# Folds of three Fourier transforms dealt out anew between VectorE and GpSimd, with their steps spread

## The chip, the cores and the metric

The kernel runs on one core of a Trainium2 chip. The metric is device microseconds (us) of one execution. Before the change three runs took 786.69, 786.71 and 786.85 us, median 786.71 us.

## The reference

Attention with a few sink tokens and a sliding window, then a Fourier mix, a normalisation and a feed-forward layer; 4 batches, 8 heads, 768 tokens, 64 features a head, model width 512, hidden width 2048, all float32.

```
scores = q @ k.T / sqrt(64);  keep = (key < n_sink) | (0 <= query - key < window)    # n_sink 4, window 128
a = softmax(where(keep, scores, -1e9));  x = heads side by side of (a @ v)           # (4, 768, 512)
u = x + real(fft(fft(x, axis=1), axis=2))
un = (u - mean(u)) / sqrt(var(u) + 1e-6)
out = u + relu(un @ w_ch1) @ w_ch2
```

## The kernel before

**Attention.** A block is 128 queries of one batch; there are 24 blocks, and each is worked in four steps of two heads. A hand-written loop runs over the steps s, and in every step each engine gets its instructions in the order of a table (SCHEDULE). Two steps' scores are issued together (TensorE, L702) into score buffers of which there are two. VectorE moves the older window's scores over (merge, L708), adds the mask and takes the maximum (soft1, L720). ScalarE takes the exponential (L726) two steps later. TensorE turns the probabilities (L751), ScalarE copies them out (pta, L758), GpSimd masks the newer and the older block (ptl at L767, pta at L775) five steps behind, and TensorE forms the products with v (xt, L789) seven steps behind. GpSimd also makes the sink weights (sk, L737 and L738), TensorE turns them (L809), ScalarE copies them (skt, L814) before a score buffer is used again. Once per block VectorE inverts the sums (L742, L743) and stores the block (L819).

**The transform.** The real part of the transform over 768 tokens and 512 features uses symmetry: before TensorE multiplies by cosines and sines, the data is folded. Of the six blocks of a batch, block j and block 3+j are added (the even token fold) and subtracted (the odd token fold, both L351), for j = 0, 1, 2. Each result is then folded over features: the even one in place (L361, the even feature fold), the odd one into the other half of the same tile (L358, the odd feature fold). ScalarE rounds the tile to its high part (gh, L364), VectorE keeps the low part (gl, L367). One middle row goes its own way: it is read from DRAM, put in place of row 0 of block 3 (put_row, L380), folded (mid_sum, L371), and split into a high and a low part (sph, mid_row, L375 and L377). Then follow the products of the first stage (L394), of the second (L421, L442), the sums d (L447, L448) and the updates of u (L458, L459), which for the first two batches are on GpSimd.

**What sets the order.** When the fourth block of batch b has been stored (step 24b + 25), fourier() enters each of its instructions in a list of events: so many steps later, on such an engine. The table SCHEDULE says where in an engine's row of a step the events stand ("V", "G", "A", "T"). For j the folds count from k = 0, 4, 8; the first stage's products begin at step 15. Up to step 97 the instructions stand on their engines as written; from there on the tile framework's scheduler orders them. The fourth transform (b = 3, called tail) has its folds on VectorE alone, and lies in that part. The first three transforms fold at about 48 to 72, 95 to 126 and 154 to 190 us.

The odd token fold has one buffer, the even one two. Instructions of one engine run in their order, so one that waits holds all behind it.

Of the kernel before, what the change touches and what calls it, by code (L numbers as in the profile page):

```python
# [25 lines left out]
NHALF = NB // 2  # L26
# [8 lines left out]
NR = 33  # L35
# [23 lines left out]
WARM = 11  # L59
WARM_STEP = (8, 0, 8, 4, 8, 4, 0)  # L60
FILL_AT, FILL = (24, 36), 0
FOLD_AT, FOLD_LAST, FOLD_ENG = (0, 4, 8), (0, 4, 8), "VG"

F_N, F_M, F_S, ROW = (3, 3), (4, 5), (6, 7), (5, 8, 10)
EV_A = 0

SINK0_AT = 3, 3, "V"
# [138 lines left out]
def kernel(  # L206
# [15 lines left out]
    V, A, G, T = nc.vector, nc.scalar, nc.gpsimd, nc.tensor  # L222

    def f32(ap):
        return ap.bitcast(F32)
# [44 lines left out]
    def run(general):  # L270
        tag = "g" if general else ""
        with ExitStack() as p1:
# [8 lines left out]
            def at(s, eng, fn):  # L281
                ev.setdefault((s, eng), []).append(fn)
# [26 lines left out]
            sph = fpool.tile([P, 384], F32R, name="sph")  # L309
# [22 lines left out]
            def fourier(b, at, ready):  # L332
# [5 lines left out]
                t_ = {}  # L338
# [9 lines left out]
                def fold_n(eng, j, odd):  # L348
                    t = fw.tile([P, DM], F32, tag=f"f{odd}", name=f"f{odd}_{b}_{j}", bufs=2 - odd)
                    t_["eo", j, odd] = t  # L350
                    eng.tensor_tensor(t, u[j], u[NHALF + j], op=ALU.subtract if odd else ALU.add)  # L351

                def fold_m(eng, j, odd):

                    g = t_["eo", j, 0]
                    if odd:
                        t = t_.pop(("eo", j, odd))
                        eng.tensor_tensor(g[:, 257:512], t[:, 1:256], t[:, 511:256:-1], op=ALU.subtract)  # L358
                        t_["g", j] = t_.pop(("eo", j, 0))
                    else:  # L360
                        eng.tensor_tensor(g[:, 1:256], g[:, 1:256], g[:, 511:256:-1], op=ALU.add)  # L361

                def fold_hi(j):
                    A.copy(gh[:, j], t_["g", j])  # L364

                def fold_lo(j):
                    V.tensor_tensor(gl[:, j], t_.pop(("g", j)), f32(gh[:, j]), op=ALU.subtract)  # L367
# [2 lines left out]
                    r = t_["x0"]  # L370
                    V.tensor_tensor(r[:, 1:256], r[:, 1:256], r[:, 511:256:-1], op=ALU.add)  # L371

                def mid_row():
                    t = t_["x0"]
                    V.tensor_copy(sph[:NR, :257], t[:, :257])  # L375
                    lo = sph[NR - 1:NR, :257]
                    V.tensor_tensor(lo, t[NR - 1:NR, :257], f32(lo), op=ALU.subtract)  # L377

# [84 lines left out]
                tail = b == B - 1 or general  # L463
                at(1, "S", load_row)
                for j in range(NHALF):
                    k = ready[j]
                    e0, e1 = FOLD_TAIL if tail else FOLD_ENG
                    eng = {"V": V, "G": G}
                    at(k + F_N[0], e0, lambda j=j: fold_n(eng[e0], j, 0))
                    at(k + F_N[1], e1, lambda j=j: fold_n(eng[e1], j, 1))  # L470
                    at(k + F_M[0], e0, lambda j=j: fold_m(eng[e0], j, 0))
                    at(k + F_M[1], e1, lambda j=j: fold_m(eng[e1], j, 1))
                    at(k + F_S[0], "A", lambda j=j: fold_hi(j))
                    at(k + F_S[1], "V", lambda j=j: fold_lo(j))
                at(ready[0] + ROW[0], "V", put_row)
                at(ready[0] + ROW[1], "V", mid_sum)
                at(ready[0] + ROW[2], "V", mid_row)
                k = ready[2] + S1
                n1, na, nb = PARTS_TAIL if tail else PARTS[b]
                for i, (kind, mc) in enumerate((("a", 0), ("a", 1), ("r", 0), ("b", 0), ("b", 1))):  # L480
# [152 lines left out]
            hp = []  # L633

            def window_attention(fourier, load_constants):
                with ExitStack() as pa:
                    kpool = pa.enter_context(tc.tile_pool(name="kpool", bufs=1, side="right"))
# [189 lines left out]
                    with ExitStack() as man:  # L827
# [130 lines left out]
                        while s < last:  # L958
# [25 lines left out]
                            for e in "AVGT":  # L984
                                for op in SCHEDULE[s >= PHASE][e][k]:
                                    if op in EVENTS:
                                        if (s, op) == (4, "G"):
                                            load_constants()
                                        run_ev(s, op)
                                    elif op in STEP_LAG:  # L990
                                        lag(table[op], s, STEP_LAG[op])
                                    else:
                                        at_ = s - BLOCK_AT[op]
                                        if at_ % NP == 0 and 0 <= at_ // NP < NQ:
                                            table[op](at_ // NP)
                                            if op == "store_x" and at_ // NP % NB == 3:
                                                b = at_ // NP // NB
                                                fourier(b, lambda d, e, f, s=s: at(s + d, e, f), FOLD_AT if b < B - 1 else FOLD_LAST)
                            s += 1
                    extra.clear()  # L1000
                return last

            def general_attention(fourier):
                for b in range(B):
                    u = uview(b)
# [331 lines left out]
```

## Time and profile before

| | |
|---|---|
| profiled execution | 786.78 us |
| its span, first to last instruction | 784.9 us |
| mean granted TensorE clock | 0.993 |
| TensorE (PE) busy | 755.2 us, 96% |
| VectorE (DVE) busy | 460.6 us, 59% |
| ScalarE (ACT) busy | 239.0 us, 30% |
| GpSimd (POOL) busy | 177.6 us, 23% |

A busy share is an average over the whole span. Attention and transforms fill the first 222 us, the feed-forward layer the rest, so the question in which stage an engine waits is answered by rows of that stage. A row of the timeline has the start in us, the duration in us, the engine, the line, the operation, output and input, and in brackets the idle time before it and what ended it. A row of the waits has who waited for whom, us in total, times and longest. A row of groups has the busy us and the mean ns behind the bar, then idle time before. Rows of one engine can overlap a little, since an instruction begins before the one ahead has drained. In a row of a stretch of time, busy times of PE, PEld (weight loads), DVE, ACT and POOL are followed by the granted clock, the DMA share and GB/s.

### The profile page before, as it was taken

What the parts mean: (1) busy time and instruction counts of PE and PEld (TensorE: products, weight loads), DVE (VectorE), ACT (ScalarE), POOL (GpSimd) and SP (SyncE); (2) the same over time, 40 slices, a digit from 0 to 9 for tenths busy, and PEclk for the clock granted to TensorE, in tenths of its full rate; (3) what the DMA queues carried; (4) which work ended last, traced back from release to release, by engine and by line L of the source; (5) the groups of instructions that cost most, each with busy time, mean ns of one, the idle gap of its engine ahead of it and who ended that gap; (6) DMA issues with size and microseconds to landing.
All of it is one profiled execution on the core that took longest, in us unless ns stands there. A gap on an engine that the chain in (4) does not pass through costs nothing.

```text
span 784.9 us, 11953 instructions
## 1 busy us (share of the span) xinstructions
PE 755.2 (96%) x4379; PEld 615.8 (78%) x4379; DVE 460.6 (59%) x1354; ACT 239.0 (30%) x704; POOL 177.6 (23%) x283
## 2 busy tenths in 40 slices
PE   7999998988899999999999999999999999999996
PEld 5666876866778878899888888888888888888895
DVE  6788687999999589561356424662456425611211
ACT  4887765756633133221111111111111110110110
POOL 2566477476645255200000000000000000000000
PEclk9999999999999999999999999999999999999999
DMA  9853525433305366120100002000200001000100
GB/s 311 251 171 109 140 84 176 127 112 99 131 27 159 111 196 210 62 71 1 54 1 0 1 9 99 1 1 0 81 1 0 1 0 54 1 1 0 55 1 32
DMA packets 41812, 57.69 MB, mean 74 GB/s; under 512 B 2796, under 2 KB 27500, under 8 KB 41360
## 3 DMA queue, kind: packets, MB, share of 16 engines
q1 hardware_dynamic: 41456, 53.07, 21.7%
q0 software_dynamic: 288, 3.76, 1.2%
q8 instruction: 37, 0.61, 0.3%
q14 instruction: 31, 0.25, 0.1%
HBM read 47.37 MB, written 9.45 MB: 72 GB/s over the span
## 4 chain that ended last, share of the span: by engine, by line
PE 80%; DVE 13%; issue 2%; POOL 1%; ACT 1%; DMA 1%; SPq 0%; DVEq 0%; ACTq 0%; POOLq 0%
PE h L619 33%; PE o L1124 33%; PE xt L789 3%; PE s L702 3%; DVE sm L720 2%; PE pt L751 2%; DVE cv L591 1%; PE za L394 1%; DVE s L708 1%; DVE cv L590 1%; PE a L421 1%; DVE cv L592 1%; DVE f L351 1%; PE x L801 1%; DMA vt<-in_v_sink_dram 1%
## 5 line engine op out<-in xcount | busy, mean ns | idle before, releaser
L1124 PE MATMUL o<-w,h 128*128 128x512 f32 x876 | 216.5, 394 | 0.0
L1117 DVE SCALAR_TENSOR_TENSOR h<-h,h 128x512 fp32r<-128x512 f32 (+1 forms) x107 | 65.4, 611 | 247.7 <-ACT h L1112 247.5
L1124 PEld LDWEIGHTS o<-w,h 128*128 128x128 f32 x876 | 162.8, 188 | 35.5
L1112 ACT ACTIVATE h<-h 128x512 fp32r<-128x512 f32 (+1 forms) x107 | 57.2, 535 | 366.4 <-PE h L619 360.1
L619 PE MATMUL h<-un_slots,w 128*128 128x512 f32 (+1 forms) x576 | 124.7, 365 | 0.0
L619 PEld LDWEIGHTS h<-un_slots,w 128*128 128x128 f32 x576 | 99.6, 188 | 19.6
L619 PE MATMUL h<-un_last,w 128*128 128x512 f32 (+1 forms) x432 | 89.0, 355 | 0.0
L619 PEld LDWEIGHTS h<-un_last,w 128*128 128x128 f32 x432 | 72.7, 188 | 12.8
L726 ACT ACTIVATE sm<-sm,mx 128x132 f32<-128x132 f32 x192 | 75.8, 400 | 7.1 <-DVE mx L720 7.1
L1148 DVE STREAM_TRANSPOSE unf<-un 32x128 f32<-32x128 f32 x224 | 67.7, 302 | 3.2
L702 PE MATMUL s<-ring,q 64*128 64x260 f32 x320 | 51.2, 422 | 12.2 <-DVE mx L720 6.4
L720 DVE CUSTOM_DVE_ANT_0 sm<-s,mask 128x132 f32<-128x132 f32 x192 | 48.7, 292 | 9.3 <-ACT skt L814 2.7
L702 PEld LDWEIGHTS s<-ring,q 64*128 64x128 f32 x320 | 27.1, 188 | 28.2 <-issue 12.4
L608 POOL TENSOR_TENSOR w<-cv,w 128x512 fp32r<-128x512 f32 x25 | 33.9, 1354 | 35.5 <-ACT w L607 35.4
L789 PE MATMUL xt<-ptl,ldv 128*64 128x128 f32 x384 | 38.9, 288 | 0.0
L708 DVE COPY_PREDICATED s<-older,s 128x256 f32<-128x256 uint8 x80 | 33.6, 420 | 7.2 <-ACT skt L814 6.8
L726 ACT ACTIVATION_READ_ACCUMULATOR sm<-sm,mx 128x1 f32 x192 | 36.8, 192 | 0.0
L1124 PE MATMUL o<-w_ring,h 128*128 128x512 f32 x144 | 35.6, 393 | 0.0
L767 POOL TENSOR_SCALAR_AFFINE_SELECT ptl<-pta 128x512 f32<-128x512 f32 x48 | 32.2, 672 | 14.4 <-ACT pta L758 14.4
L789 PEld LDWEIGHTS xt<-ptl,ldv 128*64 128x64 f32 x384 | 21.6, 137 | 14.9 <-issue 8.1
L789 PE MATMUL xt<-pta,ldv 128*64 128x128 f32 x320 | 31.7, 277 | 0.2 <-POOL pta L775 0.2
L751 PE MATMUL pt<-ident,sm 128*128 128x128 f32 x192 | 31.6, 288 | 0.0
(200 smaller groups left out, 1040.9 us busy)
## 6 DMA issues: line engine op xcount, KB each, us to landing
raw<-in_moe_w_ch_dram SPq DMA_DIRECT2D x32, 512.0 KB, 3.7
ldv<-in_v_dram SPq DMA_DIRECT2D x28, 256.0 KB, 3.6
ring<-in_qk_dram SPq DMA_DIRECT2D x24, 264.0 KB, 4.6
out_dram<-u SPq DMA_DIRECT2D x24, 256.0 KB, 3.8
q<-in_qk_dram SPq DMA_DIRECT2D x20, 256.0 KB, 4.2
cst<-in_dft_dram POOLq DMA_DIRECT2D x1, 3348.0 KB, 11.7
ud<-us SPq DMA_DIRECT2D x12, 256.0 KB, 2.2
u<-ud SPq DMA_DIRECT2D x2, 1024.0 KB, 5.1
```

The source lines that it names most:

```text
L608: G.tensor_tensor(d[1], tf, f32(d[0]), op=ALU.subtract)
L619: T.matmul(ps[:, :tb], a[:, cs], x[:, :, cc, :], start=n == 0, stop=n == 3 * NCC - 1)
L702: T.matmul(ps[:, j, :P + W], st["q", g][rows, hp, :], keys(g, 2 * hp + j), start=True, stop=True)
L708: V.copy_predicated(ps[:, :, P + NS:P + W], older[qi > 2], ps[:, :, 0:P])
L720: V.tensor_tensor_reduce(sm[:, h % 4], ps[:, j, P:P + W], mask[min(qi, 3)], -SCALE, 3.0e38, ALU.add, ALU.min, accum_out=mx[:, 0, h:h + 1])
L726: A.activation(sm[:, h % 4], sm[:, h % 4], AF.Exp, bias=mx[:, 0, h:h + 1], scale=-1.0, accum_out=mx[:, 1, h:h + 1])
L751: T.transpose(ps[:, j], sm[:, j, NS:], ident)
L789: T.matmul(ps[D * j:D * j + D, p, :], st["v", kb(g) - i][:, h, :], a[:, h % 4, :], start=i == 0, stop=i == n - 1)
L1112: A.activation(h[0], ps[:, :tb], AF.Relu)
L1117: V.scalar_tensor_tensor(h[1], ps[:, :tb], 0.0, f32(h[0]), op0=ALU.max, op1=ALU.subtract)
L1124: T.matmul(po[i], a[:, ts_], x, start=f == 0 and n == 0, stop=f == NF - 1 and n == 2)
L1148: V.transpose(unf[32 * q:32 * q + 32, :, r], un[r].rearrange("p (c q j) -> p c q j", c=NCC, q=4)[:, :, q])
```

## The change

For the first three transforms both token folds go to GpSimd and both feature folds to VectorE (before: the even ones on VectorE, the odd ones on GpSimd). The odd token fold stands one step after the even one. For j = 0 and 1 the odd feature fold, the high part and the low part come one step later than before; for j = 2 they keep their steps. The high part of the middle row goes to ScalarE, one step earlier, its low part stays on VectorE, three steps later. The fourth transform keeps its engines; its odd token fold moves by a step, and its middle row is split in the same manner.

```diff
-FOLD_AT, FOLD_LAST, FOLD_ENG = (0, 4, 8), (0, 4, 8), "VG"
-F_N, F_M, F_S, ROW = (3, 3), (4, 5), (6, 7), (5, 8, 10)
+FOLD_AT, FOLD_LAST, FOLD_ENG = (0, 4, 8), (0, 4, 8), "GV"
+F_STEPS = ((3, 4), (4, 5), (6, 7)), ((3, 4), (4, 6), (7, 8))
+ROW = 5, 8, 9, 13
...
-                def mid_row():
+                def mid_hi():
+                    A.copy(sph[:NR, :257], t_["x0"][:, :257])
+
+                def mid_lo():
                     t = t_["x0"]
-                    V.tensor_copy(sph[:NR, :257], t[:, :257])
                     lo = sph[NR - 1:NR, :257]
                     V.tensor_tensor(lo, t[NR - 1:NR, :257], f32(lo), op=ALU.subtract)
...
+                    f_n, f_m, f_s = F_STEPS[0 if tail or j == NHALF - 1 else 1]
                     e0, e1 = FOLD_TAIL if tail else FOLD_ENG
-                    at(k + F_N[0], e0, lambda j=j: fold_n(eng[e0], j, 0))
-                    at(k + F_N[1], e1, lambda j=j: fold_n(eng[e1], j, 1))
-                    at(k + F_M[0], e0, lambda j=j: fold_m(eng[e0], j, 0))
-                    at(k + F_M[1], e1, lambda j=j: fold_m(eng[e1], j, 1))
-                    at(k + F_S[0], "A", lambda j=j: fold_hi(j))
-                    at(k + F_S[1], "V", lambda j=j: fold_lo(j))
+                    at(k + f_n[0], e0, lambda j=j: fold_n(eng[e0], j, 0))
+                    at(k + f_n[1], e0, lambda j=j: fold_n(eng[e0], j, 1))
+                    at(k + f_m[0], e1, lambda j=j: fold_m(eng[e1], j, 0))
+                    at(k + f_m[1], e1, lambda j=j: fold_m(eng[e1], j, 1))
+                    at(k + f_s[0], "A", lambda j=j: fold_hi(j))
+                    at(k + f_s[1], "V", lambda j=j: fold_lo(j))
                 at(ready[0] + ROW[0], "V", put_row)
                 at(ready[0] + ROW[1], "V", mid_sum)
-                at(ready[0] + ROW[2], "V", mid_row)
+                at(ready[0] + ROW[2], "A", mid_hi)
+                at(ready[0] + ROW[3], "V", mid_lo)
```

Line numbers in the changed kernel are larger by 2 at the folds (L353 token folds, L363 and L360 feature folds, L369 low part, L381 the row's low part) and by 6 in the attention (L773, L781 masks, L743, L744 sink weights, L714 merge, L825 store).

GpSimd at the first transform's folds j = 0 and 1, before (f0 is an even fold's tile and f1 an odd one's, u0 the batch's blocks, pta and ptl the probabilities, sk the sink weights):

```order
L767 AFFINE_SELECT ptl_5_3_830<-pta_5_3_801 128x512
L351 TENSOR_TENSOR f1_0_0_832<-u0_64 128x512
L775 AFFINE_SELECT pta_5_3_801<-pta_5_3_801 128x512
L737 CAST sk_6_809<-sm_6_2_778 128x2x16
L738 TENSOR_TENSOR sk_6_809<-sm_6_2_778,sk_6_809 128x2x16
L767 AFFINE_SELECT ptl_6_1_882<-pta_6_1_860 128x512
L358 TENSOR_TENSOR f0_0_0_823<-f1_0_0_832 128x255
L737 CAST sk_7_912<-sm_7_0_826 128x2x16
L738 TENSOR_TENSOR sk_7_912<-sm_7_0_826,sk_7_912 128x2x16
L767 AFFINE_SELECT ptl_6_3_934<-pta_6_3_903 128x512
L351 TENSOR_TENSOR f1_0_1_936<-u0_64 128x512
```

And the same place now:

```order
L773 AFFINE_SELECT ptl_5_3_828<-pta_5_3_801 128x512
L353 TENSOR_TENSOR f0_0_0_830<-u0_64 128x512
L781 AFFINE_SELECT pta_5_3_801<-pta_5_3_801 128x512
L353 TENSOR_TENSOR f1_0_0_865<-u0_64 128x512
L743 CAST sk_6_809<-sm_6_2_778 128x2x16
L744 TENSOR_TENSOR sk_6_809<-sm_6_2_778,sk_6_809 128x2x16
L773 AFFINE_SELECT ptl_6_1_882<-pta_6_1_858 128x512
L743 CAST sk_7_911<-sm_7_0_824 128x2x16
L744 TENSOR_TENSOR sk_7_911<-sm_7_0_824,sk_7_911 128x2x16
L773 AFFINE_SELECT ptl_6_3_931<-pta_6_3_901 128x512
L353 TENSOR_TENSOR f0_0_1_933<-u0_64 128x512
L353 TENSOR_TENSOR f1_0_1_965<-u0_64 128x512
```

The odd token fold stands behind the older block's mask and ahead of the sink weights; the feature fold behind the next mask is gone; at j = 1 the two token folds follow one another.

VectorE at the second transform, before (the inverse of a block, then the burst of four that ends with the token fold of j = 2, then the merge):

```order
L742 TENSOR_SCALAR mx_13_1512<-mx_13_1512 128x8
L743 RECIPROCAL mx_13_1512<-mx_13_1512 128x8
L375 CAST sph_88<-xr_1_1440 33x257
L377 TENSOR_TENSOR sph_88<-xr_1_1440,sph_88 1x257
L367 TENSOR_TENSOR gl_1_1429<-f0_1_1_1654,gh_1_1428 128x512
L351 TENSOR_TENSOR f0_1_2_1778<-us_1_2_1072,us_1_5_1075 128x512
L708 COPY_PREDICATED s_15_0_1769<-older1_122,s_15_0_1769 128x2x128
```

VectorE now, one step later, behind the next step's softmax:

```order
L369 TENSOR_TENSOR gl_1_1429<-f0_1_1_1660,gh_1_1428 128x512
L363 TENSOR_TENSOR f0_1_2_1783<-f0_1_2_1783 128x255
L825 TENSOR_TENSOR u2_65<-x_12_1801,mx_12_1385 128x512
L360 TENSOR_TENSOR f0_1_2_1783<-f1_1_2_1821 128x255
L381 TENSOR_TENSOR sph_88<-xr_1_1440,sph_88 1x257
L714 COPY_PREDICATED s_15_2_1825<-older1_122,s_15_2_1825 128x2x128
```

The low part, and the row's, have moved behind the softmax of two steps, to the even feature fold and the store that stood there already, and the odd feature fold has come from GpSimd; behind the inverse only the odd feature fold of j = 1 is left.

GpSimd at the same place now (L462 and L463 are updates of the batch before):

```order
L773 AFFINE_SELECT ptl_13_3_1781<-pta_13_3_1751 128x512
L353 TENSOR_TENSOR f0_1_2_1783<-us_1_2_1069,us_1_5_1072 128x512
L781 AFFINE_SELECT pta_13_3_1751<-pta_13_3_1751 128x512
L462 TENSOR_TENSOR u0_64<-u0_64,d_0_1_1650 128x257
L463 TENSOR_TENSOR u0_64<-u0_64,d_0_1_1650 128x255
L353 TENSOR_TENSOR f1_1_2_1821<-us_1_2_1069,us_1_5_1072 128x512
L743 CAST sk_14_1759<-sm_14_2_1728 128x2x16
```

The odd token fold, which VectorE's odd feature fold of the next step reads, has been put behind the two updates.

## The prediction

> **What bounds the kernel now.** I read the page first (one core, clock 0.993), then TensorE's waits, then VectorE, GpSimd and TensorE in order of time where the three transforms fold: 48 to 72, 95 to 126 and 154 to 190 us.
>
> ```profile
> PE 755.2 (96%) x4379; PEld 615.8 (78%) x4379; DVE 460.6 (59%) x1354; ACT 239.0 (30%) x704; POOL 177.6 (23%) x283
> ...
> PE s L702 <- DVE mx L720: 4.5, 9, 2.3
> PE s L702 <- PE pt L751: 1.7, 2, 1.0
> PE s L702 <- DVE mx L742: 1.7, 4, 1.1
> PE s L702 <- DVE d L448: 1.2, 1, 1.2
> PE b L442 <- ACT asb L430: 1.0, 1, 1.0
> PE a L421 <- DVE mx L742: 0.8, 1, 0.8
> PE unx L544 <- DVE u L819: 0.7, 1, 0.7
> ```
>
> TensorE is the bound over the whole span. The waits (us in total, times, longest), taken from 48 to 190 us, add to 11.6 us: nearly all are scores waiting for VectorE to have freed a score buffer. So here VectorE sets the end, and only some 11.6 us can be won.
>
> What makes VectorE late are bursts, and GpSimd inside them. Alone, a token fold on VectorE lasts 0.64 us and a feature fold 0.42; next to GpSimd they do not:
>
> ```profile
> 48.52 0.64 DVE L351 TENSOR_TENSOR f<-u 128x512 f32<-128x512 f32 x1
> 110.78 0.42 DVE L361 TENSOR_TENSOR f<-f 128x255 f32<-128x255 f32 x1
> 115.00 0.65 DVE L375 CAST sph<-xr 33x257 fp32r<-33x257 f32 x1
> 115.69 0.74 DVE L377 TENSOR_TENSOR sph<-xr,sph 1x257 fp32r<-1x257 f32 x1
> 116.46 1.01 DVE L367 TENSOR_TENSOR gl<-f,gh 128x512 fp32r<-128x512 f32 x1
> 117.39 1.76 DVE L351 TENSOR_TENSOR f<-us,us 128x512 f32<-128x512 f32 x1
> 119.07 0.41 DVE L708 COPY_PREDICATED s<-older,s 128x256 f32<-128x256 uint8 x1
> ...
> 50.62 1.27 POOL L351 TENSOR_TENSOR f<-u 128x512 f32<-128x512 f32 x1
> 51.85 0.82 POOL L775 TENSOR_SCALAR_AFFINE_SELECT pta<-pta 128x512 f32<-128x512 f32 x1
> 52.62 0.21 POOL L737 CAST sk<-sm 128x32 fp32r<-128x32 f32 x1
> 53.77 0.72 POOL L358 TENSOR_TENSOR f<-f 128x255 f32<-128x255 f32 x1
> 116.90 1.70 POOL L351 TENSOR_TENSOR f<-us,us 128x512 f32<-128x512 f32 x1
> ```
>
> Columns are start and duration. In the second transform the fold that starts on VectorE at 117.39 ends at 119.15. GpSimd's fold ends at 118.60, and 118.60 plus about 0.6 is 119.2; GpSimd's own 1.70 is 1.27 plus what was left of VectorE's low part, 0.4 (to 116.46 + 1.01 = 117.47, where rows of one engine overlap by 0.1). So a VectorE instruction with two operands in SBUF and a GpSimd instruction take turns, whole instruction by whole instruction. [...]
>
> **The change part by part.** Over the three transforms VectorE's rows are:
>
> ```profile
> L361 DVE TENSOR_TENSOR f<-f 128x255 f32<-128x255 f32 x9 | 5.3, 592 | 0.0
> L351 DVE TENSOR_TENSOR f<-u 128x512 f32<-128x512 f32 x6 | 5.0, 832 | 0.0
> L351 DVE TENSOR_TENSOR f<-us,us 128x512 f32<-128x512 f32 x3 | 3.5, 1172 | 0.0
> L375 DVE CAST sph<-xr 33x257 fp32r<-33x257 f32 x3 | 1.4, 481 | 0.0
> ```
>
> - Removed from VectorE: nine token folds, 8.5 us with their waits (9 x 0.64 = 5.8 alone), and three casts, 1.4 us. Added: nine odd feature folds, 9 x 0.42 = 3.8 us alone. So VectorE gains between 3.4 us (5.8 + 1.4 - 3.8) and 6.1 us (8.5 + 1.4 - 3.8), before new waits.
> - GpSimd: nine odd feature folds go (0.72), nine even token folds come (1.27): 9 x 0.55 = 5.0 us more. Nine long instructions more stand in VectorE's way.
> - ScalarE: three casts of 33x257, no more than the 0.65 us of the slowest one on VectorE, one of them per transform in an engine that is busy 30%: cost between 0 and 2 us, taken at 0, since in one row alone of those above (1.0 us) TensorE waits for ScalarE. The fourth transform gets its cast off VectorE too: -0.2 us taken, 0 to -0.7.
> - New order: the odd token fold now stands a step later on GpSimd, ahead of the sink weights; the last steps of a transform put low part, even feature fold, store, odd feature fold and the middle row's low part in one row on VectorE. No DMA moves with the folds. In the part that is ordered by the scheduler, from the fourth transform on, one row load and one weight load each change places with a block's store in SP's queue; taken at 0, as three weights are kept in flight (up to one of VectorE's conversions late if they were not), and two of TensorE's products change places with their neighbours.
>
> First transform. Its rows, VectorE then TensorE:
>
> ```profile
> 51.54 0.63 DVE L361 TENSOR_TENSOR f<-f 128x255 f32<-128x255 f32 x1
> 52.70 0.40 DVE L380 COPY u<-xr 1x512 f32<-1x512 f32 x1
> 53.03 0.41 DVE L708 COPY_PREDICATED s<-older,s 128x256 f32<-128x256 uint8 x1
> 65.98 0.90 DVE L361 TENSOR_TENSOR f<-f 128x255 f32<-128x255 f32 x1
> 66.80 0.68 DVE L819 TENSOR_TENSOR us<-x,mx 128x512 f32<-128x512 f32 x1
> 67.40 0.41 DVE L708 COPY_PREDICATED s<-older,s 128x256 f32<-128x256 uint8 x1
> ...
> 54.11 0.71 PE L702 MATMUL s<-ring,q 64*128 64x260 f32 x4
> 68.58 0.71 PE L702 MATMUL s<-ring,q 64*128 64x260 f32 x4
> 120.19 0.71 PE L702 MATMUL s<-ring,q 64*128 64x260 f32 x4 [2.31 <-DVE mx L720]
> 124.90 1.15 PE L702 MATMUL s<-ring,q 64*128 64x260 f32 x8
> ```
>
> GpSimd's first fold (50.62) becomes the even one; the feature fold wanted at 51.54 waits for its end at 51.89, then for the mask of the older block, which GpSimd has started by then: 52.5. The odd fold follows on GpSimd, from about 52.8 to 54.05. The row's copy into the block (L380) overwrites what both folds read, so it cannot start before 54.05, and the merge behind it moves from 53.03 to 54.4: +1.35, which the scores at 54.11 feel. From start to start a feature fold takes 0.35 (0.42 less the overlap), the store 0.6 (66.80 to 67.40), a low part 0.6 like a token fold of its size. VectorE then skips a low part and a token fold (1.2 us) for a feature fold: 1.35 - 1.2 + 0.35 leaves 0.5 us, which I carry into the last burst. Instead of 65.98 to 67.40 (1.4 us) stand: low part 0.6 after about 0.7 of an odd token fold, even feature fold 0.35 after a sink cast (0.2), store 0.6, odd feature fold 0.35 and the row 0.35, between them a short sink instruction (0.2) and a mask (0.6): 3.95 us, +2.5. The merge of 67.40 comes at about 70.4 and the scores of 68.58 at about 71.6: **+3.0 us** (1.3 if only the row's wait stays, 4.7 if the clock drops as below).
>
> Second transform. The four VectorE rows from 115.00 take 4.07 us to 119.07; what is left there is one feature fold, so the merge comes at about 116.4, 2.7 us earlier, and TensorE's 2.31 us wait at 120.19 goes. But one step on, ScalarE's copy of the sink weights (117.25) still holds the softmax to about 118.6. [...] After today's wait the clock falls:
>
> ```profile
> 117.25 0.27 ACT L814 CAST skt<-s 128x128 fp32r<-128x128 f32 x1 [1.47 <-PE s L809]
> ...
> 120.00:122.00 2.00, 1.62 (x10) 0.69 (x10) 1.97 (x10) 1.64 (x8) 1.92 (x5) 0.85 0.00 0
> 122.00:124.00 2.00, 2.00 (x18) 1.67 (x18) 1.79 (x12) 0.00 (x0) 1.85 (x5) 0.50 0.00 0
> 124.00:126.00 2.00, 2.00 (x14) 1.30 (x14) 0.62 (x2) 1.57 (x3) 1.77 (x4) 0.79 0.43 138
> ```
>
> The column after POOL's is the granted clock: 0.85, 0.50, 0.79 over 6 us, which costs 0.3 + 1.0 + 0.4 = 1.7 us. [...] I take **-0.3 us** (-2.7 if the clock stays up, +0.7 if it falls as before). [...]
>
> Third transform. The same shape: a gain at the bursts ahead of the softmax, given back at the last one, where two updates again stand ahead of the odd token fold:
>
> ```profile
> 176.66 0.42 DVE L708 COPY_PREDICATED s<-older,s 128x256 f32<-128x256 uint8 x1
> 180.94 0.42 DVE L708 COPY_PREDICATED s<-older,s 128x256 f32<-128x256 uint8 x1
> ```
>
> The burst ahead of 176.66 loses the same four instructions as the one ahead of 119.07. Of that head start the sink copy, which holds the second step's softmax as above, leaves between 1.1 and 2.5 us (2.3 of 2.7 there). The last burst costs 2.5 more, as in the first transform, so the merge of 180.94 moves by 0 to 1.4 us: **+0.6 us**. Two refinements are left out, the statistics of the first batch that run between, and the conversions of weights behind.
>
> Sum: 3.0 - 0.3 + 0.6 - 0.2 = **+3.1 us**. The profiled execution took 786.78 us (span 784.9; the median is 786.71), so 789.9.
>
> **The rivals.** (1) Faster: GpSimd gets ahead, since it loses the feature folds that sat between its masks. If each odd token fold is over before VectorE wants it (about 1.3 us earlier than I place it), the bursts cost their price alone: the second transform keeps its 2.3 us and the 1.7 us of clock, the first loses 0.8: 786.78 - 4.0 + 0.8 = 783.6. For it: GpSimd is busy in 23% of the span. Against: in the three rows with the clock above it is busy for 1.92, 1.85 and 1.77 of 2.00 us. (2) GpSimd becomes the bound: its 5.0 us more reach TensorE through the masks, 791.8; against it, the masks run two steps ahead of their products. (3) The waits only change places, each giving back what it took: 786.8.
>
> **How the numbers follow.** The forecast has 0.42, its own range 787.6 to 792.4 (the first transform's term from 1.3 to 4.7, the third's from 0 to 1.4); rival 1 has 0.30, since the relief of VectorE is certain and the new waits are replayed; rival 2 0.12; rival 3 0.16. Within 0.2% (1.6 us) is what a measurement can't tell from no change. So slower 0.42 + 0.12 = 0.54, same 0.16, faster 0.30. The range 783.2 to 792.4 takes in rival 1 but for its lowest third and leaves out about a tenth on either side.
>
> **What would show it.** The row's copy waiting for GpSimd near 54 us; feature folds far above 0.42 us at the end of each transform; no VectorE burst and no 2.31 us wait near 118 us, but a wait at the scores two steps later. Wrong if the last-burst feature folds take 0.42, or if TensorE's waits from 48 to 190 us fall well below 11.6 us.

## The result: 7.6 us slower, and the profile after

The changed kernel takes 794.31 us in the median of five runs (792.47 to 795.54), the kernel before 786.71 beside it. The ratio is 1.0094 (95% interval 1.008 to 1.0108). The prediction said 789.9, with 783.2 to 792.4 as its range: the direction holds, the size does not. The profiled execution took 794.31 us at a granted clock of 0.987, with a span of 792.6 us (784.9 before).

The page's row of busy times first, then TensorE's waits from 48 to 200 us (us in total, times, longest):

```profile
PE 758.1 (96%) x4379; PEld 619.4 (78%) x4379; DVE 456.0 (58%) x1350; ACT 239.7 (30%) x708; POOL 181.5 (23%) x283
```

```profile
PE s L708 <- issue: 8.2, 5, 2.2
PE s L708 <- DVE mx L726: 2.0, 6, 1.1
PE unx L550 <- DVE u L825: 1.9, 1, 1.9
PE s L708 <- DMA ldv<-in_v_dram: 1.2, 1, 1.2
PE b L446 <- ACT asb L434: 1.0, 1, 1.0
PE s L708 <- DVE mx L748: 0.7, 3, 0.2
...
```

VectorE is 4.6 us less busy and GpSimd 3.9 us more, and TensorE waits longer: 15.7 us, with three rows of 0.3 us and less that are left out above, where all rows of before add to 12.0 from 48 to 200 us. That is half of the 7.7 us by which the span grew. The other half shows in the granted clock. Narrow windows find its edges; the rows below are cut at them. Columns: window and its length, busy time of PE, PEld, DVE, ACT and POOL, granted clock, then the DMA share and rate.

```profile
69.44:72.85 3.41, 1.47 (x10) 0.66 (x8) 3.25 (x14) 2.25 (x7) 2.31 (x5) 1.00 0.77 245
72.85:76.27 3.42, 3.42 (x25) 3.04 (x24) 1.00 (x6) 0.21 (x2) 0.00 (x0) 0.50 0.46 149
124.05:127.47 3.42, 1.35 (x18) 0.94 (x14) 2.76 (x10) 2.61 (x8) 3.27 (x6) 1.00 0.48 126
127.47:130.88 3.41, 3.29 (x20) 2.25 (x22) 2.94 (x12) 0.72 (x4) 3.12 (x7) 0.50 1.00 342
171.84:175.25 3.41, 1.54 (x18) 1.30 (x14) 3.38 (x10) 1.67 (x6) 1.69 (x4) 1.00 0.30 113
175.25:178.67 3.42, 3.23 (x15) 2.54 (x15) 2.53 (x11) 2.14 (x6) 2.84 (x5) 0.50 0.28 81
185.49:188.90 3.41, 1.30 (x10) 0.68 (x8) 3.38 (x11) 2.67 (x8) 3.26 (x7) 1.00 0.54 167
188.90:192.32 3.42, 2.55 (x18) 1.91 (x20) 3.28 (x12) 0.00 (x0) 2.00 (x2) 0.50 0.19 69
192.32:195.73 3.41, 3.41 (x17) 2.98 (x14) 1.65 (x10) 1.62 (x7) 0.03 (x1) 0.50 0.54 170
216.21:219.62 3.41, 1.78 (x11) 1.70 (x12) 3.41 (x7) 0.46 (x1) 2.23 (x3) 1.00 0.12 47
219.62:223.03 3.41, 2.42 (x26) 1.90 (x24) 3.41 (x6) 1.98 (x5) 2.80 (x3) 1.00 0.79 281
```

The clock falls to 0.50 for whole windows of 3.41 us, each of which costs at most 1.7 us of TensorE. The edges lie on one grid: from 72.85 to 127.47 are 16 windows of 3.414 us, to 175.25 another 14, to 188.90 another 4. Each of the first four pairs has TensorE busy for less than half of a window (1.30 to 1.54 of 3.41 us), and the next window at 0.50. Between 48 and 780 us there are five such windows; before there were two, at 121.41 and 210.15. The five are worth up to 4 x 1.7 + 1.3 = 8.1 us (the one with PE busy for 2.55 us counts half of that), the two 3.4, so 4.7 us more. With the 3.7 us of waits that is 8.4, against 7.7 seen; the rest is not parted further.

The places are those that the prediction looked at. VectorE's rows at the first transform, then TensorE's and GpSimd's (start, duration):

```profile
52.12 0.83 DVE L363 TENSOR_TENSOR f<-f 128x255 f32<-128x255 f32 x1 [0.30 <-POOL f L353]
54.11 0.41 DVE L384 COPY u<-xr 1x512 f32<-1x512 f32 x1 [0.56 <-POOL f L353]
54.46 0.41 DVE L714 COPY_PREDICATED s<-older,s 128x256 f32<-128x256 uint8 x1
...
66.16 0.43 DVE L714 COPY_PREDICATED s<-older,s 128x256 f32<-128x256 uint8 x1 [1.17 <-ACT skt L820]
67.06 1.05 DVE L369 TENSOR_TENSOR gl<-f,gh 128x512 fp32r<-128x512 f32 x1
68.03 0.42 DVE L363 TENSOR_TENSOR f<-f 128x255 f32<-128x255 f32 x1
68.38 0.68 DVE L825 TENSOR_TENSOR us<-x,mx 128x512 f32<-128x512 f32 x1
68.98 0.45 DVE L360 TENSOR_TENSOR f<-f 128x255 f32<-128x255 f32 x1
69.46 0.73 DVE L381 TENSOR_TENSOR sph<-xr,sph 1x257 fp32r<-1x257 f32 x1
70.23 0.43 DVE L714 COPY_PREDICATED s<-older,s 128x256 f32<-128x256 uint8 x1
...
71.32 0.71 PE L708 MATMUL s<-ring,q 64*128 64x260 f32 x4 [1.71 <-issue]
...
52.65 1.43 POOL L353 TENSOR_TENSOR f<-u 128x512 f32<-128x512 f32 x1
```

The row's copy waits for GpSimd's odd token fold and starts at 54.11 (forecast 54.05); the merge behind it comes at 54.46 (forecast 54.4); the merge behind the last burst at 70.23 (forecast 70.4), the scores at 71.32 (forecast 71.6). Less the 0.2 us by which the changed kernel is late already at 40 us, from its loading, the replay was right to 0.5 us. Part of that is luck: the last burst began 0.9 us late, where 0.5 was carried into it (ScalarE's copy of the sink weights holds the merge at 66.16), and took 3.2 us from 67.06 to the merge, where 3.95 was forecast. What the replay did not carry into the sum is the clock after 72.85.

The starts of the stores of a block (the multiply into the block) show by how much the changed kernel is late, less that 0.2 us: 1.4 us ahead of the last burst of the first transform (66.80 before, 68.38 after), 4.1 behind it (73.54, 77.84). In the second transform the lateness falls to 3.0 (121.19, 124.36) and is 4.1 again behind it (129.36, 133.63). In the third it is 4.7 (168.51, 173.41), then 3.8 ahead of the last burst (179.68, 183.68), then 8.1 (198.43, 206.70). First transform +4.1, second 0, third +4.0, the rest -0.6.

The last bursts of the second and third transform, with the scores behind them:

```profile
123.50 0.94 DVE L363 TENSOR_TENSOR f<-f 128x255 f32<-128x255 f32 x1
125.60 0.42 DVE L360 TENSOR_TENSOR f<-f 128x255 f32<-128x255 f32 x1 [0.56 <-POOL f L353]
183.32 0.43 DVE L363 TENSOR_TENSOR f<-f 128x255 f32<-128x255 f32 x1
184.28 0.45 DVE L360 TENSOR_TENSOR f<-f 128x255 f32<-128x255 f32 x1
186.20 0.42 DVE L714 COPY_PREDICATED s<-older,s 128x256 f32<-128x256 uint8 x1
...
127.59 2.18 PE L708 MATMUL s<-ring,q 64*128 64x260 f32 x8 [2.19 <-issue]
```

### The profile page after: what moved, and what is told of

Same layout as the page of the kernel before. It is cut to its first block, busy times and chain, and to the rows that moved or that the text cites. A ratio compares the mean times of both kernels' runs of the same rounds, so it can differ in the third digit from the quotient of the medians.

```text
span 792.6 us, 11970 instructions
## 1 busy us (share of the span) xinstructions
PE 758.1 (96%) x4379; PEld 619.4 (78%) x4379; DVE 456.0 (58%) x1350; ACT 239.7 (30%) x708; POOL 181.5 (23%) x283
## 4 chain that ended last, share of the span: by engine, by line
PE 77%; DVE 16%; issue 2%; ACT 1%; DMA 1%; POOL 1%; SPq 1%; DVEq 0%; ACTq 0%; POOLq 0%
PE o L1130 32%; PE h L625 32%; PE xt L795 4%; PE s L708 3%; DVE sm L726 2%; DVE cv L597 2%; PE pt L757 2%; DVE s L714 2%; PE za L398 2%; DVE cv L598 1%; DVE cv L596 1%; DMA vt<-in_v_sink_dram 1%; DVE gl L369 1%; PE zr L398 1%; PE x L807 1%
## 5 line engine op out<-in xcount | busy, mean ns | idle before, releaser
L1130 PE MATMUL o<-w,h 128*128 128x512 f32 x876 | 216.5, 394 | 0.0
L614 POOL TENSOR_TENSOR w<-cv,w 128x512 fp32r<-128x512 f32 x25 | 36.2, 1449 | 35.2 <-ACT w L613 35.0
L714 DVE COPY_PREDICATED s<-older,s 128x256 f32<-128x256 uint8 x80 | 33.7, 421 | 17.2 <-ACT skt L820 14.4
L773 POOL TENSOR_SCALAR_AFFINE_SELECT ptl<-pta 128x512 f32<-128x512 f32 x48 | 33.0, 688 | 13.8 <-ACT pta L764 13.8
```

Source lines behind the costliest of these rows:

```text
L614: G.tensor_tensor(d[1], tf, f32(d[0]), op=ALU.subtract)
L714: V.copy_predicated(ps[:, :, P + NS:P + W], older[qi > 2], ps[:, :, 0:P])
L1130: T.matmul(po[i], a[:, ts_], x, start=f == 0 and n == 0, stop=f == NF - 1 and n == 2)
```

## The experiments

Theory A: the last burst of each transform stops TensorE for 1.7 to 2.2 us, and the stop costs a window of slow clock on top. Rivals: B, the spread steps and the split row cost the time whichever engine folds; C, GpSimd's load does; and, of the clock, that slow windows only fill time in which TensorE would have waited for VectorE. All ratios are against the kernel before on the same chip (medians 786.92 to 787.31 us). The edits are shown shortened, most of them in the names of the kernel before, and "..." marks what is left out.

**Filling the waits.** TensorE gets products that nobody reads: at step 40 6 of them ahead of the scores, at step 64 7, at step 88 6 ahead of the scores and 4 between them. They go into a PSUM tile of the transform's products at steps 40 and 64, and into one of the turned probabilities at step 88, where the filler itself waits 0.73 us for ScalarE to have copied that tile.

```diff
+FILLS = {40: ((0, 6),), 64: ((0, 7),), 88: ((0, 6), (1, 4))}
...
 if s % 2 == 0:
+    for where, n in FILLS.get(s, ()):
+        if where == 0:
+            fill_in(s, n)
     lag(scores, s, 0)
+    for where, n in FILLS.get(s, ()):
+        if where == 1:
+            fill_in(s, n)
     lag(scores, s, -1)
```

> The changed kernel, with TensorE kept busy in three of its waits: 6 transposes of the identity ahead of the scores that wait near 70 us, 7 ahead of those near 126 us, 6 and 4 ahead of and between those near 187 us (products that nobody reads, some 0.16 us each, 1.0 to 1.2 us in a wait of 1.7 to 2.2 us). Theory A: the granted clock stays at 1.00 there, and of the 6.8 us of TensorE time that the four dips of 1.7 us cost (one at 72, one at 128, two at 188 to 196), 4 to 6 us come back, the rest being waited out later: 788.5 to 790.5. Rival (the slow clock only fills time in which TensorE would have waited for VectorE anyway): 794.3, within 0.8, or up to 1 us more where a filler delays a score.

Measured: 789.73 us, ratio 1.0032 (1.0019 to 1.0046). That is 4.6 us less than the changed kernel, and inside the forecast of theory A. The same windows, on this run's grid:

```profile
70.52:73.93 3.41, 2.13 (x18) 1.20 (x17) 3.28 (x15) 1.98 (x6) 2.03 (x5) 1.00 0.85 261
73.93:77.35 3.42, 3.42 (x34) 3.17 (x31) 1.94 (x11) 1.88 (x9) 0.21 (x1) 1.00 0.41 134
125.13:128.54 3.41, 1.71 (x13) 0.80 (x12) 3.06 (x14) 1.65 (x6) 3.26 (x7) 1.00 0.93 292
128.54:131.96 3.42, 3.42 (x23) 3.09 (x23) 2.82 (x9) 0.49 (x2) 1.37 (x3) 0.50 0.97 379
186.57:189.98 3.41, 2.51 (x23) 1.55 (x24) 3.41 (x15) 1.01 (x5) 3.34 (x4) 1.00 0.35 135
```

Where the filler lifts a window to 2.13 or 2.51 us of work, the next stays at 1.00; where it reaches 1.71 only, the next falls. The work of VectorE and GpSimd is untouched, and 4.6 of the 7.6 us come back, so most of the loss is the clock, not the lateness itself. The profiled run is one of the two slowest of seven, 791.26 us; there 3.1 us come back, with two slow windows between 48 and 780 us in place of five.

**The last burst.** The row's low part goes one step on; or the last of the three folds goes back to the engines and steps of before.

```diff
-ROW = 5, 8, 9, 13
+ROW = 5, 8, 9, 14
```

> The changed kernel, with the row's low part one step later (14 for 13), out of the step in which the odd feature fold and the merges of the last burst stand. Theory A: each last burst is 0.35 to 0.74 us shorter, so the waits of 1.71, 2.19 and 1.91 us come to 1.0 to 1.8 us: 0.4 to 0.7 us of wait for each transform, and a dip of 1.7 us for each wait that falls below about 1.45 us: 788.5 to 792.5. Rival (the low part only fills time in which VectorE waits for GpSimd's odd token fold): 794.3, within 0.8.

Measured: 788.06 us, ratio 1.001 (1.0 to 1.0021): 6.2 us of the 7.6 gone with one instruction per transform moved one step, 0.4 more than theory A allowed; the rival falls. VectorE and TensorE at the first transform:

```profile
68.77 0.45 DVE L360 TENSOR_TENSOR f<-f 128x255 f32<-128x255 f32 x1
69.14 0.42 DVE L714 COPY_PREDICATED s<-older,s 128x256 f32<-128x256 uint8 x1
71.77 0.42 DVE L381 TENSOR_TENSOR sph<-xr,sph 1x257 fp32r<-1x257 f32 x1
...
70.21 0.71 PE L708 MATMUL s<-ring,q 64*128 64x260 f32 x4 [0.80 <-PE pt L757]
```

The merge follows the odd feature fold at once, the wait is 0.80 for 1.71 us, and the low part costs 0.42 here where it met GpSimd for 0.73. The waits of 1.71, 2.19 and 1.91 us are 0.80, 1.63 and 0.69 here (forecast 1.0 to 1.8). No slow window stands at the first and third transform of this run, one at the second (126.26).

```diff
-f_n, f_m, f_s = F_STEPS[0 if tail or j == NHALF - 1 else 1]
+last_j = not tail and j == NHALF - 1
+f_n, f_m, f_s = ((3, 3), (4, 5), (6, 7)) if last_j else F_STEPS[0 if tail else 1]
-e0, e1 = FOLD_TAIL if tail else FOLD_ENG
+e0, e1 = FOLD_TAIL if tail else ("VG" if last_j else FOLD_ENG)
...
+en, em = (e1, e0) if last_j else (e0, e1)
```

> The changed kernel, with only the last of the three folds of each transform put back to the engines and steps of before (even folds on VectorE, odd ones on GpSimd, 3, 3 / 4, 5 / 6, 7); the first two folds and the row as changed. Theory A: the odd feature fold leaves the last burst, so TensorE's waits near 70, 126 and 187 us fall below 1.4 us and most of the dips behind them go; what stays is the row's copy waiting near 54 us (+1.4) and a part of the third transform: 787.5 to 790.5. Rival (GpSimd's load and the first two folds make the loss): 792.5 to 795.

Measured: 788.59 us, ratio 1.0017 (1.0001 to 1.0033). The forecast of theory A; theory C falls for the changed kernel, since two of three folds still load GpSimd as the change does. The three waits are 0.74, 1.88 and 0.73 us: the middle one stayed, and with it its slow window.

**The row's copy.**

```diff
-ROW = 5, 8, 9, 13
+ROW = 7, 8, 9, 13
```

> The changed kernel, with the row's copy into the block two steps later (step 7 for 5), where the odd token fold that it overwrites is long over. Theory A: the copy's wait near 54 us and the waits of 1.2 us at 55 and 62 us go, 0.5 to 1.4 us of the first transform; the last burst and its waits stay, so 792.5 to 794; if the wait at 70 us then falls below 1.4 us its dip goes as well, 791 to 792.5. Rival (the copy hides the fold's lateness, which then shows at the next feature fold): 794.3, within 0.8.

Measured: 795.19 us, ratio 1.0101 (1.0086 to 1.0116): nothing is won, as the rival said (0.1 us above its range). The copy no longer waits and the merge comes earlier (53.12 for 54.46, of which 0.3 is the loading), but the next fold's even feature fold now meets GpSimd's two token folds for 1.48 us (0.42 in the changed kernel), and TensorE waits 0.17 and 2.03 us at the scores where it waited 1.21 and 1.15:

```profile
53.12 0.41 DVE L714 COPY_PREDICATED s<-older,s 128x256 f32<-128x256 uint8 x1
58.64 1.48 DVE L363 TENSOR_TENSOR f<-f 128x255 f32<-128x255 f32 x1
...
62.05 0.71 PE L708 MATMUL s<-ring,q 64*128 64x260 f32 x4 [2.03 <-issue]
```

**Engines, steps and row by themselves.** Three kernels on the folds of before, and the engine swap alone:

```diff
-FOLD_ENG = "VG"
+FOLD_ENG = "GV"
...
-at(k + F_N[1], e1, lambda j=j: fold_n(eng[e1], j, 1))
-at(k + F_M[0], e0, lambda j=j: fold_m(eng[e0], j, 0))
+at(k + F_N[1], e0, lambda j=j: fold_n(eng[e0], j, 1))
+at(k + F_M[0], e1, lambda j=j: fold_m(eng[e1], j, 0))
```

> Only the engines change against the kernel before: both token folds on GpSimd, both feature folds on VectorE, at the old steps (3, 3 / 4, 5 / 6, 7), and the middle row stays in one piece on VectorE at step 10. Theory A (waits and clock): the last burst of each transform keeps its odd feature fold but loses the row's low part (0.42 to 0.74 us), so TensorE's waits of 1.7 to 2.2 us at the scores shrink to 1.0 to 1.6 us; where they still pull the granted clock to 0.50 the loss stays at 6 to 8 us (792.5 to 794.5), where they no longer do it falls to 2 to 4 us (788.5 to 791). Theory B (the spread steps and the split row make the loss): no change from before, 786.7, within 0.8. Theory C (GpSimd's load of nine even token folds is the bound): 793 to 795, since the load is the same.

Measured: 792.39 us, ratio 1.0066 (1.0053 to 1.0079). Theory B falls as the whole cause: with the old steps and the row in one piece, the swap costs 5.2 us. The time is 0.1 us under theory A's upper case and 0.6 under theory C's, and its trace (790.25 us, the fastest of the six) fits neither alone: it has two slow windows like the kernel before, so its 3.5 us there are not more slow windows but mostly waits, 14.9 us for 12.0 from 48 to 200 us. Among them TensorE does wait for GpSimd's masks, 1.4 us in two waits.

```diff
-F_N, F_M, F_S, ROW = (3, 3), (4, 5), (6, 7), (5, 8, 10)
+F_STEPS = ((3, 4), (4, 5), (6, 7)), ((3, 4), (4, 6), (7, 8))
+ROW = 5, 8, 9, 13
```

> Only the steps and the row change against the kernel before: even folds stay on VectorE and odd folds on GpSimd, but at the new steps (3, 4 / 4, 5 or 4, 6 / 6, 7 or 7, 8), with the row's cast on ScalarE at step 9 and its low part on VectorE at step 13. Theory A: no odd feature fold stands on VectorE in the last burst and the row's copy waits for one GpSimd fold that starts a step later, so at most +1.5 us, and the burst that held TensorE 2.31 us near 120 us loses its row, which can give 1.7 us of clock back: 785 to 788. Theory B: 793 to 795. Theory C: as before, 786 to 788.

Measured: 787.51 us, ratio 1.0006 (0.9996 to 1.0016): no difference. Theory B falls here too (793 to 795); A and C both allowed this time.

```diff
-F_N, F_M, F_S, ROW = (3, 3), (4, 5), (6, 7), (5, 8, 10)
+F_N, F_M, F_S, ROW = (3, 3), (4, 5), (6, 7), (5, 8, 9, 14)
...
-at(ready[0] + ROW[2], "V", mid_row)
+at(ready[0] + ROW[2], "A", mid_hi)
+at(ready[0] + ROW[3], "V", mid_lo)
```

> The kernel before with its folds as they were; only the middle row's piece is split: its cast on ScalarE at step 9, its low part on VectorE at step 14, a step in which VectorE waits for GpSimd in the trace of before (1.38 us at 125.5 us). The row's two instructions (0.65 + 0.74 us) leave the burst from 115 to 119 us. Theory A: the scores' wait of 2.31 us at 120 us falls to 0.9 to 1.4 us and its dip of 1.7 us goes, 1.0 to 3.1 us less than before: 783.8 to 786. Rival (ScalarE's copy of the sink weights at 117.25 us holds the softmax anyway, and the wait only moves a step on): as before, within 0.8.

Measured: 783.04 us (782.12 to 783.61), ratio 0.9943 (0.9927 to 0.996). This beats both kernels, by more than theory A forecast. Behind the shortened burst the merge and the scores stand at

```profile
116.77 1.12 DVE L351 TENSOR_TENSOR f<-us,us 128x512 f32<-128x512 f32 x1
117.81 0.41 DVE L711 COPY_PREDICATED s<-older,s 128x256 f32<-128x256 uint8 x1
118.93 0.71 PE L705 MATMUL s<-ring,q 64*128 64x260 f32 x4 [0.66 <-DVE mx L723]
```

where before they stood at 119.07 and 120.19, with a wait of 2.31 us and the slow window behind it. In the profiled run no window between 20 and 778 us is slow. The gain does not come from the second transform alone, to which the forecast kept: with the 0.3 us by which this run is late at 40 us taken off, the store at 139 us comes 0.9 us earlier than before and the one at 198 us 3.4.

```diff
 F_STEPS = ((3, 4), (4, 5), (6, 7)), ((3, 4), (4, 6), (7, 8))
-ROW = 5, 8, 9, 13
+ROW = 5, 8, 9, 14
 FOLD_ENG = "VG"
```

> The engines of before (even folds on VectorE, odd ones on GpSimd) with the spread steps of the change, the row's cast on ScalarE at step 9 and its low part on VectorE at step 14. It parts the steps from the engines in the 5.0 us between the changed kernel with its row at step 14 (788.06) and the kernel before with its row at step 14 (783.04). If the engine swap alone costs them, and the spread steps are free: 783.0, within 1. If the spread steps cost them: 786.5 to 788. If the low part's step 13 was the whole price of the earlier trial of the steps (787.5), this comes out below 784.5 too.

Measured: 785.16 us, ratio 0.9983 (0.9972 to 0.9995), between the two forecasts. So the parts of the change are, in medians (each beside a median of 786.7 to 787.3 us for the kernel before):

| folds | row in one piece, step 10 | low part at 13 | low part at 14 |
|---|---|---|---|
| engines and steps of before | 787.2 | not run | 783.04 |
| engines of before, spread steps | not run | 787.51 | 785.16 |
| engines swapped, steps of before | 792.39 | not run | not run |
| engines swapped, spread steps | not run | 794.31 | 788.06 |

The row's split gains 4.2 us at step 14; spreading the steps takes back 2.1 and swapping the engines 2.9; step 13 in place of 14 costs 2.4 us with the old engines and 6.2 with the new, where it falls on the last burst. The prices hold for these steps of the table only: by itself, on the old steps and with the row in one piece, the swap costs 5.2, not 2.9.

**The third transform alone.**

```diff
+new = tail or b == 2
-f_n, f_m, f_s = F_STEPS[0 if tail or j == NHALF - 1 else 1]
+f_n, f_m, f_s = F_STEPS[0 if tail or j == NHALF - 1 else 1] if new else ((3, 3), (4, 5), (6, 7))
-e0, e1 = FOLD_TAIL if tail else FOLD_ENG
+e0, e1 = FOLD_TAIL if tail else ("GV" if new else "VG")
...
```

> The whole change in the third transform alone (folds, steps and the row of the third; the first two as before; the fourth as after). If the losses add by transform, as the stores say (+4.1, about 0, +4.0, rest -0.6): 790.1, with TensorE waiting near 170 and 184 us and the granted clock at 0.50 behind each wait. If the third's loss needs the lateness that the first two hand on: 786 to 788. Theory B would put it at +2 to +3, 789, with the wait at the row's low part.

Measured: 788.85 us, ratio 1.0025 (1.0013 to 1.0036): +1.7, between the first two forecasts and next to theory B's 789, which has a part here, since the row's low part stands at step 13. Its third transform has one slow window (at 185.5 us) where the changed kernel has three (175.25, 188.90, 192.32): TensorE waits 1.87 us at 169.69 as it does at 174.14 after, but no window of this run's grid holds enough of that wait. By the stores its third transform costs 2.2 us where the changed kernel's costs 4.0, so the other 1.8 us would be windows that fall by the place of the grid; that is argued from two traces, not tried. That each run has its own grid is shown by the edges of 72.85 and 73.93 in the rows above.

**Fillers in the other kernels.** Three more, each with 5 or 7 transposes ahead of waiting products; `fill` as above.

```diff
+if s == 62: warm_up(7, fill)                 # kernel before
+if b == 2 and kind == "b" and mc == 1: warm_up(7, fill)
```

> The kernel before, with TensorE kept busy in its two long waits: 7 transposes that nobody reads ahead of the scores that wait 2.31 us at 120 us, and 7 ahead of the sine products that wait 2.05 us at 209.6 us (1.2 us each time). Theory A (a wait of about 1.5 to 2.3 us costs a dip of 3.5 us at a granted clock of 0.50, 1.7 us of TensorE, on top of itself): both dips go, 2.0 to 3.4 us less than before, 783.5 to 785. Rival (the dips only fill time that would be waited anyway): same as before, within 0.8.

Measured: 790.69 us, ratio 1.0043 (1.0029 to 1.0056): a miss of the forecast by 6 us. The first filler did its part (stores were 1.0 us late ahead of it and 0.3 early behind it). The second stands where the scheduler sets the order, and new waits stand behind it:

```profile
PE dc L428 <- DVE zb L416: 3.1, 2, 2.8
PE za L401 <- ACT gh L369: 2.6, 1, 2.6
```

Both are followed by a slow window (216.5 and 237 us). Which instruction the scheduler moved wasn't pursued.

> The kernel before with the first filler of the earlier trial alone: 7 transposes that nobody reads ahead of the scores that wait 2.31 us at 120 us. There the stores behind 130 us came 1.3 us earlier against those ahead of it. Theory A: the dip at 121.5 us goes and nothing else changes, 1.3 to 1.7 us less: 785.0 to 786.0. Rival: the transposes delay the scores as much as the clock gains: as before, within 0.8.

Measured: 787.07 us, ratio 0.999 (0.9978 to 1.0003): the rival's number, but the interval reaches down to 1.7 us less, so theory A is not shut out. Near 120 us the wait is 0.2 us and the clock 1.00, but in the profiled run the scores at 108 us waited 1.94 us for a load of values, with a slow window behind. Its runs spread from 784.94 to 788.63.

> The changed kernel with the row's low part one step later (14 for 13) and 5 transposes that nobody reads (0.8 us) ahead of the scores that still wait 1.63 us at 124 us there. Theory A: the dip at 126.5 us goes as well, 1.3 to 1.7 us less than the 788.06 of that kernel without them: 786.2 to 787. Rival: 788, within 0.8.

Measured: 787.89 us, ratio 1.0008 (0.9995 to 1.0021), no difference from the same kernel without the filler, as the rival said. The window behind 124 us is at 1.00 in the profiled run: against the kernel without the filler its store at 121.8 us is 0.25 us late and the one at 139.2 us 1.3 us early. The medians of 12 runs don't show that gain, and why is open. So of the four trials with fillers one, in the changed kernel, shows in the medians what the clock costs.

## Why the prediction was wrong in size

**Right.** VectorE and GpSimd hold each other up: a feature fold beside GpSimd takes 0.83 us (52.12; 0.42 alone), GpSimd's fold beside VectorE 1.43 (52.65; 1.27 alone), as replayed. The row's copy waits where it was said. The bursts of the second transform shrink and its wait moves to the scores of two steps later (2.31 us at 120.19 before, 2.19 at 127.59 now), slow window and all, so the term is 0 for the -0.3 forecast. No run shows that -0.3, an estimate of the author: by the stores the changed kernel is 4.1 us late ahead of the second transform and 4.1 behind it. GpSimd did not become the bound: no wait of TensorE for its masks is among the rows above. And the waits, without the clock, come out at the sum: the merge behind the last burst is 2.6 us late in the first transform (+3.0 forecast), the second transform costs nothing, the merge of 180.94 comes at 186.20, 1.0 us later than the 4.1 before it (+0.6 forecast, from 0 to 1.4), and the rest is -0.6: 3.0 us for the 3.1 of the forecast. That the sum is so near is partly luck, since its terms are off by 0.3 to 0.4 us in both directions.

**Wrong: the clock was kept out of the sum.** This is the step that failed. The first transform's term of +3.0 named the drop as its upper end (4.7) only; it came, and between the merge at 70.23 and the store at 77.84 the lateness grew from 2.6 to 4.1. The third transform's term of +0.6 had no drop even in its range of 0 to 1.4; there the two windows at 188.90 and 192.32 took it from +1.0 at the merge to +4.0. The prediction had the row for it, 0.85, 0.50 and 0.79 behind a wait of 2.31 us, and itself forecast the late scores at 71.6 us and the 2.5 us longer last burst of the third transform, but added no clock to either. Together that is 1.5 + 3.0 = 4.5 us, about the distance from 789.9 to 794.31. The fillers agree in direction: with them the changed kernel lost 2.6 us (789.73 for 787.16) in the median, and 4.5 in the profiled run (791.26 for 786.78), where both kernels have two slow windows and the fillers' own delays are in the sum.

**Wrong: the sign of the last bursts.** The prediction was to be wrong if the feature folds of the last burst took 0.42 us. They did: 0.42 and 0.45 in the first transform, 0.43 and 0.45 in the third; only the second had one of 0.94 and one of 0.42 behind a wait of 0.56 for GpSimd. So the late scores do not come from feature folds that GpSimd holds up. They come from the number of instructions ahead of the merge, and GpSimd holds up the low part (1.05 us at 67.06, 0.64 alone at 72.35) and the row's low part (0.73 us at 69.46; 0.42 alone at 71.77 with the row at step 14). Rival 1 asked that each odd token fold be over before VectorE wants it; in the last bursts of the first and third transform it was (over at 67.57, wanted at 68.98; over at 182.18, wanted at 184.28), and the gain did not come even so.

**The third transform, +0.6 forecast, +4.0 measured.** Both halves of "a gain at the bursts ahead, given back at the last one" came: the lateness falls from 4.7 to 3.8 us ahead of the last burst. It would have fallen more, but the products of the first batch wait behind the store,

```profile
174.14 0.66 PE L550 MATMUL unx<-ident,un 128*128 128x128 f32 x4 [1.87 <-DVE u L825]
184.76 0.74 DVE L381 TENSOR_TENSOR sph<-xr,sph 1x257 fp32r<-1x257 f32 x1
187.99 0.71 PE L708 MATMUL s<-ring,q 64*128 64x260 f32 x4 [1.91 <-issue]
189.77 1.24 PE L708 MATMUL s<-ring,q 64*128 64x260 f32 x4 [1.08 <-DVE mx L726]
```

a wait of 0.7 us before, and the window behind it, at 175.25, is slow; with the change in the third transform alone, where that window is not slow, the lateness falls by 1.6 us. These are the first batch's statistics that the prediction named as left out. Then the last burst stopped the scores for 1.91 us, where it was 0.95 before, and the two windows behind it are slow; the second wait, 1.08 us, was there before as well (1.05).

**Not seen: the place of the row's low part.** It stands right ahead of the merges in the last burst and meets GpSimd there, 0.73 and 0.74 us where 0.35 and two waits were replayed. The burst as a whole was priced too high, not too low (3.95 for 3.2 us in the first transform); what was missed is that one instruction less ahead of the merge leaves TensorE enough work in its window to keep the clock, in the first and third transform: 2.38 us from 68.23 and 2.92 from 184.29 with the row at step 14, where the changed kernel has 1.47 and 1.30 on its own grid and loses the next window. Moving it one step won 6.2 us, the dearest single choice of the change. In the other direction, the row taken off the bursts of the kernel before is worth 4.2 us by itself; the prediction had bounded the gain at the burst of 115 us, for the second transform, at 2.7, and asked it of no other.

**Right place, no price: the row's copy, +1.35.** Without its wait the kernel is no faster (795.19): GpSimd's folds then hold the next feature fold, and TensorE waits as long one pair of scores later.

## What to carry to other kernels

Price a stop of the bounding engine with the clock that follows it: add up TensorE's work in stretches of 3.4 us around each new wait, and where 1.9 us or less is left, add up to 1.7 us (all three as measured on this kernel: in the six traces below the clock fell to 0.50 for a window of 3.41 us every time that up to 1.54 us was left, and in some cases up to 1.86). Then look at what stands between the late instruction and the one that frees the buffer it waits for: here one step for an instruction of 0.4 to 0.7 us that nobody was waiting for moved the time by 6.2 us. A table of the parts (engines, steps, row) shows when a good part of a change is hidden by a bad one.

## What the runs showed of the hardware

In six traces (the kernel before, the changed one, the engines alone, the steps alone, the fillers in the changed kernel, the row at step 14) the slow windows between 48 and 240 us start a whole number of windows of 3.41 us apart: 26 from 121.41 to 210.15 before, 17 from 128.18 to 186.21 and 8 more to 213.52 with the steps alone. The grid does not start at the same place in each run (edges at 72.85 in the changed kernel, at 73.93 with the fillers). Cut along these grids, a window at full clock with TensorE busy for up to 1.54 us was followed by one at 0.50, one with 2.0 us or more by 1.00; in between both came (1.71 us at 125.13 with the fillers and 1.86 at 124.77 with the steps alone were followed by 0.50, 1.78 us at 216.21 in the changed kernel by 1.00). At half clock 2.55 us were not enough to come back (188.90 in the changed kernel). So two waits can add up. The kernel with the spread steps alone had waits of only 0.75 and 0.88 us, both in one window, and lost the next:

```profile
182.80:186.21 3.41, 1.78 (x15) 0.86 (x15) 3.41 (x16) 2.37 (x7) 3.33 (x6) 1.00 0.34 94
186.21:189.62 3.41, 3.41 (x24) 3.08 (x23) 2.20 (x8) 0.56 (x2) 2.80 (x4) 0.50 0.21 77
```

And one wait may cost nothing: the same wait of 2.05 or 2.06 us at the sine products near 210 us was followed by a slow window in four of eight traces (the kernel before, the one with the first filler alone, the row at step 14 with and without its filler), in four not (the changed kernel, the row's copy at step 7, the row alone, the steps with the row at 14). Which waits fall into one window is so a matter of the run, which may be why the changed kernel's five runs spread by 3.1 us: the fastest, 792.47 us, has a mean clock of 0.992, the slowest two, 795.51 and 795.54, 0.984 and 0.983. That the grid makes this difference was not tried.

VectorE's instructions with both operands in SBUF and GpSimd's took turns beyond the folds too. In the changed kernel's trace a step of the weights' conversion lasts 1.67 us from 248.39, where GpSimd is busy up to 249.51, and 0.69 from 288.19, where one operand lies in PSUM, though GpSimd is busy from 287.48 to 288.78. A single operand in SBUF did not spare the row's cast before: 0.65 us at 115.00, 0.23 at 62.21 without GpSimd beside it.
